# Tile 6 normalised ahead of tile 3, z sum 0 behind its rstd, and four x loads moved in SP's queue: linear attention beside a SwiGLU block on one core

## The chip, the cores and the metric

The kernel runs on one core of one Trainium2 chip. The time is the device time of one execution in microseconds. TensorE (PE) multiplies, VectorE (DVE), ScalarE (ACT) and GpSimd (POOL) do the elementwise work, and SyncE (SP) issues nearly all DMAs. Each engine works through its own list of instructions in order; semaphores make one wait for another.

## The reference: what is computed

The input x has 2048 rows of 512 features. Its rows are normalised, and two branches work on the result: linear attention with 32 heads of 16 features, and a SwiGLU network of width 1792. The output is x plus both.

```python
phi = lambda t: jnp.where(t > 0, t + 1, jnp.exp(t)) + 1e-6
xn = _layernorm(x, axis=-1)
q, k, v = split(xn @ wqkv)               # 32 heads of 16
pq, pk = phi(q), phi(k)
kv  = einsum("bhsd,bhse->bhde", pk, v)   # a sum over all rows
z   = einsum("bhsd->bhd", pk)            # a sum over all rows
o   = einsum(pq, kv) / (einsum(pq, z)[..., None] + 1e-6)
out = x + o @ wo + (silu(xn @ w_gate) * (xn @ w_up)) @ w_down
```

## The kernel before

The 2048 rows are 16 tiles of 128 rows. The first stage goes over the tiles and takes about the first 48 us of the span; the second, the feed-forward part and the output, takes the rest. The edit lies in the first stage, between 10 and 22 us.

For a tile t of the first stage:

- SP loads x (L204). Tiles 0 to 5 come alone, the others in pairs: 6/7, 8/9, 10/11, 12/13, 14/15.
- Statistics: `bns` (L297) and `agg` (L300) on VectorE give mean and variance; `eps` (L325) and `rstd_of` (L334) on GpSimd give 1/sqrt(variance + 1e-5). Each of the latter two is an instruction on one element per partition. `stat(t)` stands for the four of them.
- `xn_dve` (L314) on VectorE normalises the tile. `xn(t)` is `xn_dve(t)` with `transpose_dma(t)` (L408) behind it: SP issues a DMA that writes the transposed tile to xnT. For tile 6 of the kernel before, the two are written apart.
- `kproj`, `qproj` (L417) on TensorE: four matmuls each, with the transposed tile as weights.
- Features of k: ACT takes the exponential from the matmul's bank (L465), VectorE clips it (L484, `clip_k`) and adds the positive part (L493, `maxadd_k`).
- `gtacc` (L569) on TensorE: four matmuls that add the product of the normalised tile and its features, called G here, into four banks. The normalised tile is the weights, so they wait for `xn_dve(t)` and for the features.
- `zsum(t)` on GpSimd adds the features to zacc (L561). `zsum(0, 0)` is a copy with a change of type (L557), a "cast" in the profile.

Tiles 0 to 3 go another way, so that TensorE can begin early: their projections (L431, L444) use the tile less its mean, and ACT applies rstd afterwards (L501, L507, L519); VectorE adds the two parts of the features (L533, `first_feat`). So xn of tile 3 is needed for G only.

The order is written out by hand. A call of `K.op` or `K.dma` appends an instruction to its engine's list and works out from the names it reads and writes which semaphores it waits for. So a call that stands further up moves an instruction ahead in that engine's list alone, past everything there. TensorE's list around the edit is: G of tiles 1 and 2, k and q projections of tile 4, G of 3, projections of 5, G of 4, projections of 6, G of 5, projections of 7. From tile 5 on, a loop repeats the pattern; its statistics of tiles 10 to 15 come in the steps `STAT = {5: (10,), 6: (11,), 7: (12,), 8: (13, 14), 9: (15,)}`.

VectorE's list from the features of tile 3 on is, before the change: `first_feat(3)`, `xn_dve(3)`, `bns(7)`, `xn_dve(6)`, `agg(7)`, `bns(8)`, `agg(8)`, `clip_k(4)`, `xn_dve(7)`, `maxadd_k(4)`. GpSimd's is `rstd_of(5)`, `zsum(0, 0)`, `eps(6)`, `rstd_of(6)`, `eps(7)`, `rstd_of(7)`. SP's is the transpose of xc for tile 3, x 8/9, T4, x 10/11, T5, x 12/13, x 14/15, T6, T7, where Tn is the transpose of tile n.

Of the kernel before, what the change touches and what calls it, by code (L numbers as in the profile page):

```python
# [108 lines left out]
def bass_parallel_sum__linear_attn_block__swiglu_ffn__prompt_kernel(  # L109
# [13 lines left out]
    pe, act, dve, pool, sp = nc.tensor, nc.scalar, nc.vector, nc.gpsimd, nc.sync  # L123
    bf, f32 = dt.bfloat16, dt.float32

    with contextlib.ExitStack() as es:
# [63 lines left out]
        def bk(i):  # L190
            return ("bank", i)
# [5 lines left out]
        def rows(v, t0, n):  # L197
            if t0 < NLONE:
                return v[t0 * P:(t0 + n) * P, :].rearrange("(t p) d -> p t d", p=P)
            return v[NLONE * P:, :].rearrange("(p t) d -> p t d", t=NT - NLONE)[:, t0 - NLONE:t0 - NLONE + n, :]  # L200

        def xload(eng, h, t0, n, after=()):
            K.dma(
                eng, lambda: h.dma_start(x_sb[:, t0:t0 + n, :], rows(xin, t0, n)),  # L204
                r=list(after), w=[("x", t0 + i) for i in range(n)],
            )
# [89 lines left out]
        def bns(t):  # L296
            K.op("dve", lambda: dve.bn_stats(stats[:, t, :], x_sb[:, t, :]), r=[("x", t)], w=[("st", t)])  # L297

        def agg(t):
            K.op("dve", lambda: dve.bn_aggr(mv[:, t, :], stats[:, t, :]), r=[("st", t)], w=[("mv", t)])  # L300
# [10 lines left out]
        def xn_dve(t):  # L311
            K.op(
                "dve",
                lambda: dve.tensor_scalar(  # L314
                    out=xn_sb[:, t, :], in0=x_sb[:, t, :], scalar1=mv[:, t, 0:1], scalar2=rstd[:, t:t + 1],
                    op0=ALU.subtract, op1=ALU.mult,
                ),
                r=[("x", t), ("mv", t), ("rstd", t)], w=[("xn", t)],
            )

        def eps(t, eng):
            h = dve if eng == "dve" else pool
            K.op(
                eng,
                lambda: h.tensor_scalar(  # L325
                    out=vpe[:, t:t + 1], in0=mv[:, t, 1:2], scalar1=1e-5, scalar2=None, op0=ALU.add,
                ),
                r=[("mv", t)], w=[("vpe", t)],
            )

        def rstd_of(t):
            K.op(
                "pool",
                lambda: pool.tensor_tensor(out=rstd[:, t:t + 1], in0=vpe[:, t:t + 1], in1=nhalf[:, :], op=ALU.pow),  # L334
                r=[("vpe", t), ("nhalf",)], w=[("rstd", t)],
            )
# [40 lines left out]
        def transpose_xc(t):  # L377
            K.dma(
                "sp",
                lambda: sp.dma_start_transpose(out=xcT[:, NDC * t:NDC * (t + 1), :], in_=xc_sb[:, t, :]),  # L380
                r=[("xc", t, 0), ("xc", t, 1)], w=[("xcT", t, 0), ("xcT", t, 1)],
            )
# [22 lines left out]
        def transpose_dma(t):  # L405
            K.dma(
                "sp",
                lambda: sp.dma_start_transpose(out=xnT[:, :, t * P:(t + 1) * P], in_=xn_sb[:, t, :]),  # L408
                r=[("xn", t)], w=[("xnT", t)],
            )  # L410
# [29 lines left out]
        def proj_part(t, wname, c, pos):  # L440
            lo, b = (D, kb(t)) if wname == "wk" else (0, qb(t))
            K.op(
                "pe",
                lambda: pe.matmul(  # L444
                    banks[b], xcT[:, NDC * t + c, :], wqkv_sb[:, c, lo:lo + D],
                    start=(pos == 0), stop=(pos == NDC - 1),
                ),
                r=[("xcT", t, c // 2), (wname, c)], w=[bk(b)],
            )

        def kb(t):
            return 2 * (t % 2)

        def qb(t):
            return 2 * (t % 2) + 1

        def kproj(t):
            proj(t, kb(t), D, "wk")
# [10 lines left out]
        def exp_q(t):  # L469
            K.op(  # L470
                "act", lambda: act.activation(eq[:, t, :], banks[qb(t)], ACT.Exp),
                r=[bk(qb(t))], w=[("eq", t)],
            )

        def copy_q(t):
            K.op(
                "act", lambda: act.activation(pkq[:, t, 1, :], banks[qb(t)], ACT.Copy),
                r=[bk(qb(t))], w=[("pq", t)],
            )
# [25 lines left out]
        def first_pk(t):  # L505
            K.op(
                "act", lambda: act.activation(kpos[:, t % NE, :], banks[kb(t)], ACT.Relu, scale=rstd[:, t:t + 1]),  # L507
                r=[bk(kb(t)), ("rstd", t)], w=[("kpos", t % NE)],
            )
# [20 lines left out]
        def first_feat(t):  # L530
            K.op(
                "dve",
                lambda: dve.tensor_tensor(out=pkq[:, t, 0, :], in0=kpos[:, t % NE, :], in1=ek[:, t % NE, :], op=ALU.add),  # L533
                r=[("kpos", t % NE), ("ek", t % NE)], w=[("pk", t)],
            )

        def clip_k(t):
            clip(ek[:, t % NE, :], ("ek", t % NE))
# [14 lines left out]
        def zsum(t, e):  # L553
            pk = pkq[:, t, 0, :]
            after = [] if e is None else [("ek", e)]
            if t == 0:
                K.op("pool", lambda: pool.tensor_copy(zacc[:, :], pk), r=[("pk", t)] + after, w=[("zacc",)])  # L557
            else:
                K.op(
                    "pool",  # L560
                    lambda: pool.tensor_tensor(out=zacc[:, :], in0=zacc[:, :], in1=pk, op=ALU.add),  # L561
                    r=[("pk", t), ("zacc",)] + after, w=[("zacc",)],
                )

        def gtacc(t):
            K.op(
                "pe",
                [
                    (lambda c=c: pe.matmul(  # L569
                        banks[4 + c], xn_sb[:, t, c * P:(c + 1) * P], pkq[:, t, 0, :],  # L570
                        start=(t == 0), stop=(t == NT - 1),
                    ))
                    for c in range(NDC)
                ],
                r=[("xn", t), ("pk", t)], w=[bk(4 + c) for c in range(NDC)],
            )
# [7 lines left out]
        def xn(t):  # L584
            xn_dve(t)
            if t >= 3:
                transpose_dma(t)
# [43 lines left out]
        proj_part(1, "wq", 1, 1)  # L631
        transpose_xc(3)
        xload("sp", sp, 8, 2)
        proj_part(0, "wq", 0, 0)
        proj_part(0, "wq", 1, 1)
        first_pk(0)
# [25 lines left out]
        eps(4, "pool")  # L662
        rstd_of(4)
        xn(4)
        xload("sp", sp, 10, 2)
        agg(5)
        first_pk(1)
        first_feat(1)
# [9 lines left out]
        rstd_of(3)  # L678
        rstd_of(5)
        xn(5)  # L680
        xload("sp", sp, 12, 2)
        xload("sp", sp, 14, 2)
        bns(6)
        first_pq(2)
        proj_first(3, "wk", 1)
        first_ek(3)
        clip_k(3)
        zsum(0, 0)
        first_pk(3)
        agg(6)  # L690
        eps(6, "pool")
        first_feat(3)
        gtacc(1)
        gtacc(2)
        xn_dve(3)
        bns(7)
        kproj(4)
        rstd_of(6)
        xn_dve(6)
        agg(7)  # L700
        eps(7, "pool")
        rstd_of(7)
# [2 lines left out]
        qproj(4)  # L705
        stat(8)
        exp_q(4)
        transpose_dma(6)
        copy_q(4)
        clip_k(4)  # L710
        zsum(1, 1)
# [339 lines left out]
```

## Time and profile before

| | |
|---|---|
| median of 3 runs | 212.25 us (211.96 to 212.31) |
| the profiled execution's own time | 212.38 us |
| its span, from first to last instruction | 211.1 us |
| TensorE busy | 206.5 us, 98% |
| VectorE, ACT, GpSimd busy | 119.6, 70.9, 74.2 us |
| granted TensorE clock | 1.000 |

All stretches and instructions below come from the one profiled execution and are counted from the start of its span. A row of the timeline reads: start, duration, engine, line of the kernel, operation, output and inputs, shape, count, and in brackets how long the engine had been idle and what released it. PEld is TensorE's loading of weights, SPq the issue of a DMA by SP; the issue ends before the data have landed.

### The profile page before, as it was taken

What the parts mean: (1) busy time and instruction counts of PE and PEld (TensorE: products, weight loads), DVE (VectorE), ACT (ScalarE), POOL (GpSimd) and SP (SyncE); (2) the same over time, 40 slices, a digit from 0 to 9 for tenths busy, and PEclk for the clock granted to TensorE, in tenths of its full rate; (3) what the DMA queues carried; (4) which work ended last, traced back from release to release, by engine and by line L of the source; (5) the groups of instructions that cost most, each with busy time, mean ns of one, the idle gap of its engine ahead of it and who ended that gap; (6) DMA issues with size and microseconds to landing.
All of it is one profiled execution on the core that took longest, in us unless ns stands there. A gap on an engine that the chain in (4) does not pass through costs nothing.

```text
span 211.1 us, 2755 instructions
## 1 busy us (share of the span) xinstructions
PE 206.5 (98%) x968; PEld 95.3 (45%) x987; DVE 119.6 (57%) x246; ACT 70.9 (34%) x125; POOL 74.2 (35%) x95
## 2 busy tenths in 40 slices
PE   8999899999999999999999999999999999999996
PEld 3443444445444444444444444444444444444444
DVE  3989889434464775546374746464656535374222
ACT  4787466976443331213122312112032213121000
POOL 3638887749032444122140432231414031221200
DMA  6757444795694011210202011202021010210201
GB/s 209 202 146 162 79 99 83 201 375 191 169 363 89 3 25 25 50 25 28 51 0 50 12 33 32 50 0 50 3 50 25 26 25 28 33 44 25 50 25 53
DMA packets 30288, 16.84 MB, mean 80 GB/s; under 512 B 20929, under 2 KB 29633, under 8 KB 30273
## 3 DMA queue, kind: packets, MB, share of 16 engines
q1 hardware_dynamic: 29984, 16.39, 29.2%
q10 hardware_dynamic: 288, 0.26, 0.4%
q8 instruction: 8, 0.13, 0.3%
q14 instruction: 8, 0.06, 0.1%
HBM read 9.70 MB, written 2.10 MB: 56 GB/s over the span
## 4 chain that ended last, share of the span: by engine, by line
PE 89%; DVE 4%; DMA 3%; ACT 2%; issue 1%; POOL 1%; DVEq 0%
PE psum L771 44%; PE psum L954 23%; PE psum L417 8%; PE psum L943 7%; PE psum L569 4%; DMA xnT<-xn_sb 2%; PE psum L444 2%; DMA x_sb<-in_A_x_dram 1%; DVE pkq L533 1%; ACT ek L501 1%; ACT pkq L519 1%; PE psum L389 1%; DVE stats L297 1%; ACT kpos L507 1%; POOL prod L901 1%
## 5 line engine op out<-in xcount | busy, mean ns | idle before, releaser
L786 ACT ACTIVATE sg<-psum 128x512 bf16<-128x512 f32 x56 | 33.4, 598 | 106.8 <-PE psum L771 104.9
L771 PE MATMUL psum<-xnT,wg_sb 128*128 128x512 bf16 x222 | 57.4, 379 | 0.1
L771 PE MATMUL psum<-xnT,wu_sb 128*128 128x512 bf16 x217 | 56.0, 379 | 0.4
L901 POOL TENSOR_TENSOR prod<-pkq,zb 128x512 f32<-128x512 bf16 x16 | 18.6, 1160 | 57.8 <-DVE pkq L493 57.8
L771 PEld LDWEIGHTS psum<-xnT,wu_sb 128*128 128x128 bf16 x224 | 21.9, 98 | 26.4
L771 PEld LDWEIGHTS psum<-xnT,wg_sb 128*128 128x128 bf16 x224 | 21.9, 98 | 26.2
L967 DVE TENSOR_TENSOR out_sb<-psum,x_sb 128x512 bf16<-128x512 f32 (+2 forms) x17 | 11.2, 660 | 35.9 <-PE psum L954 35.9
L925 POOL TENSOR_TENSOR pqn<-pkq,rden 128x512 bf16<-128x512 bf16 x16 | 16.9, 1055 | 36.6 <-DVE rden L919 36.6
L792 DVE TENSOR_TENSOR pkq<-psum,sg 128x512 bf16<-128x512 f32 x28 | 19.1, 687 | 18.6 <-PE psum L771 14.1
L792 DVE TENSOR_TENSOR xn_sb<-psum,sg 128x512 bf16<-128x512 f32 x28 | 18.8, 672 | 14.2 <-PE psum L771 13.6
L954 PE MATMUL psum<-wd_sb,xn_sb 128*128 128x512 bf16 (+2 forms) x123 | 25.4, 355 | 0.2
L954 PE MATMUL psum<-wd_sb,pkq 128*128 128x512 bf16 x110 | 25.2, 379 | 0.1
L417 PE MATMUL psum<-wqkv_sb,xnT 128*128 128x512 bf16 x94 | 22.3, 379 | 0.9 <-DMA xnT<-xn_sb 0.8
L561 POOL TENSOR_TENSOR zacc<-zacc,pkq 128x512 f32<-128x512 f32 x15 | 17.3, 1155 | 5.1 <-DVE ek L484 4.6
L954 PEld LDWEIGHTS psum<-wd_sb,xn_sb 128*128 128x128 bf16 x126 | 11.8, 98 | 12.5
L954 PEld LDWEIGHTS psum<-wd_sb,pkq 128*128 128x128 bf16 x112 | 10.9, 98 | 13.2
L943 PE MATMUL psum<-m_sb,eq 128*128 128x512 bf16 (+2 forms) x67 | 16.5, 366 | 0.1
L569 PE MATMUL psum<-pkq,xn_sb 128*128 128x512 bf16 x63 | 15.9, 379 | 0.1
L417 PEld LDWEIGHTS psum<-wqkv_sb,xnT 128*128 128x128 bf16 x96 | 9.3, 98 | 12.4 <-DMA xnT<-xn_sb 1.3
L909 DVE TENSOR_REDUCE den<-prod 128x32 f32<-128x512 f32 x16 | 10.9, 683 | 5.7 <-POOL prod L901 5.7
L297 DVE BATCH_NORM_STATS2 stats<-x_sb 128x6 f32<-128x512 bf16 x16 | 10.9, 679 | 3.4 <-DMA x_sb<-in_A_x_dram 3.3
L493 DVE SCALAR_TENSOR_TENSOR pkq<-pkq,eq 128x512 bf16<-128x512 bf16 x16 | 11.1, 692 | 0.6
(65 smaller groups left out, 142.2 us busy)
## 6 DMA issues: line engine op xcount, KB each, us to landing
out_dram<-out_sb SPq DMA_DIRECT2D x15, 128.0 KB, 1.7
wg_sb<-in_B_w_gate_dram SPq DMA_DIRECT2D x2, 896.0 KB, 7.8
wu_sb<-in_B_w_up_dram SPq DMA_DIRECT2D x2, 896.0 KB, 6.0
wd_sb<-in_B_w_down_dram SPq DMA_DIRECT2D x1, 1792.0 KB, 9.7
x_sb<-in_A_x_dram SPq DMA_DIRECT2D x5, 256.0 KB, 3.1
x_sb<-in_A_x_dram SPq DMA_DIRECT2D x5, 128.0 KB, 3.3
wqkv_sb<-in_A_wqkv_dram SPq DMA_DIRECT2D x5, 128.0 KB, 3.4
wqkv_sb<-in_A_wqkv_dram SPq DMA_DIRECT2D x1, 512.0 KB, 7.6
```

What stands on the lines that cost most here:

```text
L297: K.op("dve", lambda: dve.bn_stats(stats[:, t, :], x_sb[:, t, :]), r=[("x", t)], w=[("st", t)])
L417: (lambda c=c: pe.matmul(banks[b], xnT[:, c, t * P:(t + 1) * P], wqkv_sb[:, c, lo:lo + D], start=(c == 0), stop=(c == NDC - 1),))
L561: lambda: pool.tensor_tensor(out=zacc[:, :], in0=zacc[:, :], in1=pk, op=ALU.add),
L569: (lambda c=c: pe.matmul(banks[4 + c], xn_sb[:, t, c * P:(c + 1) * P], pkq[:, t, 0, :], start=(t == 0), stop=(t == NT - 1),))
L771: (lambda c=c: pe.matmul(banks[b], w_sb[:, c, fc * P:(fc + 1) * P], xnT[:, c, C * 512:(C + 1) * 512], start=(c == 0), stop=(c == NDC - 1),))
L786: lambda: act.activation(sg[:, j % NSG, :], banks[gb], ACT.Silu),
L792: lambda: dve.tensor_tensor(out=hT(C, fc), in0=banks[ub], in1=sg[:, j % NSG, :], op=ALU.mult,),
L901: lambda: pool.tensor_tensor(out=p, in0=pkq[:, t, 1, :], in1=zb[:, :], op=ALU.mult),
L925: lambda: pool.tensor_tensor(out=pqn[:, t % NPN, :].rearrange("p (h e) -> p h e", e=DH), in0=pkq[:, t, 1, :].rearrange("p (h e) -> p h e", ...
L943: (lambda g=g: pe.matmul(dst, pqnT(t)[:, g, :], m_sb[:, g, lo:hi], start=(g == 0), stop=False,))
L954: (lambda fc=fc: pe.matmul(dst, hT(C, fc)[:, jj * P:(jj + 1) * P], wd_sb[:, fc, lo:hi], start=False, stop=(fc == NFC - 1),))
L967: lambda: dve.tensor_tensor(out=o, in0=src, in1=x_sb[:, t, lo:hi], op=ALU.add),
```

## The change

Five edits in the order of calls; no instruction is added or taken away.

- The load of x 10/11 goes from behind T4 to behind x 8/9.
- The load of x 12/13 goes from behind T5 to behind T4.
- The load of x 14/15 goes from behind T5 to behind T6.
- `rstd_of(6)` and the normalisation of tile 6 go ahead: on GpSimd eps 6 and rstd 6 stand ahead of `zsum(0, 0)`, on VectorE xn 6 stands directly behind `first_feat(3)`, ahead of xn 3 and `bns(7)`.
- The transpose of tile 6 is issued directly behind its normalisation. On SP it keeps its place between T5 and T7.

```diff
         transpose_xc(3)
         xload("sp", sp, 8, 2)
+        xload("sp", sp, 10, 2)
...
         xn(4)
-        xload("sp", sp, 10, 2)
+        xload("sp", sp, 12, 2)
...
         xn(5)
-        xload("sp", sp, 12, 2)
-        xload("sp", sp, 14, 2)
         bns(6)
...
         clip_k(3)
-        zsum(0, 0)
         first_pk(3)
         agg(6)
         eps(6, "pool")
+        rstd_of(6)
+        zsum(0, 0)
         first_feat(3)
         gtacc(1)
         gtacc(2)
+        xn(6)
+        xload("sp", sp, 14, 2)
         xn_dve(3)
         bns(7)
         kproj(4)
-        rstd_of(6)
-        xn_dve(6)
         agg(7)
...
         exp_q(4)
-        transpose_dma(6)
         copy_q(4)
```

## Prediction

> **What bounds the kernel now.** I read the page first, then who waited for whom on TensorE, then the chain that ended last, then the timeline of each engine from 8 to 26 us, where the edit lies.
>
> ```profile
> span 211.1 us, 2755 instructions
> PE 206.5 (98%) x968; PEld 95.3 (45%) x987; DVE 119.6 (57%) x246; ACT 70.9 (34%) x125; POOL 74.2 (35%) x95
> ```
>
> ```profile
> PE psum L417 <- DMA xnT<-xn_sb: 0.8, 1, 0.8
> ```
>
> TensorE is busy nearly all the time, so the only thing that an order of the other engines can win is TensorE's idle time. The list of waits on TensorE has one inside the work: 0.8 us, a projection (L417) that waits for a transposed tile. The chain and TensorE's rows show which tile.
>
> ```profile
> 17.19 0.41 DVE xn_sb L314
> ...
> 17.63 4.04 DMA xnT<-xn_sb
> ```
>
> ```profile
> 15.57 1.89 PE L417 MATMUL psum<-wqkv_sb,xnT 128*128 128x512 bf16 x8
> 17.30 1.03 PE L569 MATMUL psum<-pkq,xn_sb 128*128 128x512 bf16 x4
> 18.16 1.89 PE L417 MATMUL psum<-wqkv_sb,xnT 128*128 128x512 bf16 x8
> 19.89 1.03 PE L569 MATMUL psum<-pkq,xn_sb 128*128 128x512 bf16 x4
> 21.71 1.90 PE L417 MATMUL psum<-wqkv_sb,xnT 128*128 128x512 bf16 x8 [0.80 <-DMA xnT<-xn_sb]
> 24.31 1.89 PE L417 MATMUL psum<-wqkv_sb,xnT 128*128 128x512 bf16 x8
> ```
>
> In the order of the code these are the projections of tile 4 (15.57), G of tile 3 (17.30), projections of 5, G of 4 (19.89), projections of 6 (21.71) and of 7 (24.31). Eight matmuls follow each other in 1.73 us (18.16 to 19.89), so four take 0.86, and tile 6 could have begun at 19.89 + 0.86 = 20.75. It began at 21.71: **0.96 us** are to be won at most (the view says 0.8, because the last matmul before the gap drains). The transpose of tile 6 (T6) was issued at 17.63, right behind the normalisation of tile 6 (17.19 to 17.60), and needed 4.04 us.
>
> **The loads (edits to SP's queue).** SP's rows, and what a transpose and a load take to land:
>
> ```profile
> 10.25 0.57 SPq L204 DMA_DIRECT2D x_sb<-in_A_x_dram  x1
> 11.78 1.20 SPq L408 DMA_TRANSPOSE xnT<-xn_sb  x1
> 13.03 0.58 SPq L204 DMA_DIRECT2D x_sb<-in_A_x_dram  x1
> 14.20 1.20 SPq L408 DMA_TRANSPOSE xnT<-xn_sb  x1
> 15.44 1.05 SPq L204 DMA_DIRECT2D x_sb<-in_A_x_dram  x2
> ```
>
> ```profile
> x_sb<-in_A_x_dram SPq DMA_DIRECT2D x2, 256.0 KB, 3.1
> xnT<-xn_sb SPq DMA_TRANSPOSE x1, 2.7
> ```
>
> ```profile
> xnT<-xn_sb SPq DMA_TRANSPOSE x16, 2.5
> ```
>
> x 10/11 move from behind T4 to behind x 8/9: SP issues them from 10.82 to 11.39 in idle time, before T4 at 11.78. T4 then has two loads ahead of it in place of one. T5, one load ahead, took 2.7 against the usual 2.5, so bounds for T4 are 0 and, if it must wait out the whole second load's place, 0.57 us: it lands by 11.78 + 2.5 + 0.57 = 14.85. Its projection begins at 15.57, so this costs nothing; the cover is 0.7 us. x 12/13 take the place of x 10/11 ahead of T5, which sees what it sees now. x 14/15 go behind T6: two loads (15.44, 3.1 us each) that now lie ahead of T6 are gone, one lies ahead of T7. x 10 to 13 land earlier than now; x 14/15 land near 18.5 + 3.1 = 21.6 and are read in steps 8 and 9 of the loop, behind the projections of tile 7 (24.31): no reader waits.
>
> **Tile 6 forward, z sum 0 back (edits to VectorE and GpSimd).** The rows of VectorE, then GpSimd's, then the weight loads of G of tiles 3 and 4:
>
> ```profile
> 13.16 0.69 DVE L533 TENSOR_TENSOR pkq<-kpos,ek 128x512 bf16<-128x512 f32 x1
> ...
> 15.02 0.17 DVE L300 BATCH_NORM_AGGREGATE mv<-stats 128x2 f32<-128x6 f32 x1
> 15.39 0.94 DVE L533 TENSOR_TENSOR pkq<-kpos,ek 128x512 bf16<-128x512 f32 x1 [0.19 <-ACT kpos L507]
> 16.25 0.40 DVE L314 TENSOR_SCALAR xn_sb<-x_sb,mv,rstd 128x512 bf16<-128x512 bf16 x1
> 16.58 0.68 DVE L297 BATCH_NORM_STATS2 stats<-x_sb 128x6 f32<-128x512 bf16 x1
> ...
> 17.52 0.18 DVE L300 BATCH_NORM_AGGREGATE mv<-stats 128x2 f32<-128x6 f32 x1
> ...
> 18.73 0.41 DVE L314 TENSOR_SCALAR xn_sb<-x_sb,mv,rstd 128x512 bf16<-128x512 bf16 x1
> 19.06 0.68 DVE L493 SCALAR_TENSOR_TENSOR pkq<-psum,ek 128x512 bf16<-128x512 f32 x1
> ...
> 23.46 0.29 DVE L484 TENSOR_SCALAR ek<-ek 128x512 bf16<-128x512 bf16 x1 [0.44 <-ACT ek L465]
> ```
>
> ```profile
> 15.18 0.61 POOL L557 CAST zacc<-pkq 128x512 f32<-128x512 bf16 x1 [1.52 <-DVE ek L484]
> 15.76 0.65 POOL L325 TENSOR_SCALAR vpe<-mv 128x1 f32<-128x1 f32 x1
> 16.50 0.58 POOL L334 TENSOR_TENSOR rstd<-vpe,nhalf 128x1 f32<-128x1 f32 x1
> 17.78 0.22 POOL L325 TENSOR_SCALAR vpe<-mv 128x1 f32<-128x1 f32 x1 [0.70 <-DVE mv L300]
> 18.09 0.61 POOL L334 TENSOR_TENSOR rstd<-vpe,nhalf 128x1 f32<-128x1 f32 x1
> ```
>
> ```profile
> 17.08 0.75 PEld L569 LDWEIGHTS psum<-pkq,xn_sb 128*128 128x128 bf16 x4
> ...
> 19.80 0.62 PEld L569 LDWEIGHTS psum<-pkq,xn_sb 128*128 128x128 bf16 x4 [0.24 <-DVE pkq L493]
> ```
>
> Nothing is added or removed on VectorE; the normalisation of tile 6 (xn 6) goes ahead of that of tile 3 and of the statistics of tile 7. What counts is when it can run, for all behind it in VectorE's queue waits with it. Call its end **e**.
>
> Step 1, rstd 6. Tile 6's aggregate ends at 15.19, so eps 6 starts near 15.28 and rstd 6, 0.31 behind as with tile 7 (17.78, 18.09), near 15.59. There it meets the features of tile 3, from 15.39 on. The z sum's cast no longer runs beside these, so I give them 0.69 as at 13.16, not 0.94: they end at 16.08. Today eps 6 lies beside them and takes 0.65 in place of 0.22, ending 0.08 behind them (16.41 against 16.33). So the bounds for rstd 6 are 15.59 + 0.61 = 16.20 (not held) and 16.08 + 0.08 + (0.61 - 0.22) = 16.55 (held until the features let go). I take 16.55, the nearest row being that of eps 6.
>
> Step 2, the cast. Z sum 0 now stands right behind rstd 6 on GpSimd and waits for nothing else; GpSimd starts the next instruction 0.03 before the last ends (15.76 against 15.79), so it runs from 16.52 to 17.13. VectorE starts xn 6 some 0.11 after rstd 6 (17.08 to 17.19), at 16.66, when the cast is already running. What such a meeting costs is shown further down the trace:
>
> ```profile
> 35.04 1.24 DVE L314 TENSOR_SCALAR xn_sb<-x_sb,mv,rstd 128x512 bf16<-128x512 bf16 x1
> ```
>
> ```profile
> 34.97 1.16 POOL L561 TENSOR_TENSOR zacc<-zacc,pkq 128x512 f32<-128x512 f32 x1
> ```
>
> A normalisation that meets a z sum already running took 1.24 in place of 0.40 us and ended 0.15 behind it. So xn 6 has the bounds 16.66 + 0.40 = 17.06 and 17.13 + 0.15 = **17.28**; I take 17.28, since the features at 15.39 were also lengthened beside this very cast (0.94, not 0.69). The Trainium skill, "SBUF — State Buffer", section "Who interferes with whom", says that VectorE in a two-port mode and GpSimd exclude each other for a whole instruction and that issue order, not the kind of instruction, decides who is blocked. The row at 35.04 agrees; without that rule both meetings would cost nothing, the sum below would be a gain of 0.83, and putting the cast right behind rstd would be harmless.
>
> Step 3, behind xn 6. Xn 3 starts 0.07 before its forerunner ends, as bns 7 does now (16.58 against 16.65): 17.21 to 17.61. G of tile 3 takes xn 3 as weights; with 0.06 to the weight load and 0.09 to the matmul (as at 19.74, 19.80, 19.89) it begins at 17.76, 0.46 later than now. Bns 7 begins at 17.54 and the aggregate of tile 7 0.68 later at 18.22, 0.70 later than 17.52. The rest of the queue up to the features of tile 4 keeps its order, so these end at 19.74 + 0.70 = 20.44, and G of tile 4 begins at 20.44 + 0.15 = 20.59 (TensorE alone would be there at 19.89 + 0.46 = 20.35). Tile 6 follows at 20.59 + 0.86 = **21.45**.
>
> Step 4, T6. It is issued at 17.28 + 0.03 = 17.31 and lands at 19.8 with 2.5 us, or at 21.35 with today's 4.04: in time either way. So the wait for T6 goes, and VectorE's features of tile 4 take its place.
>
> **Sum.** 21.71 - 21.45 = 0.26 us earlier; in general 17.54 - e. Nothing gives it back later: at 23.46 VectorE has waited 0.44 us for ACT, so its 0.70 is caught up within two tiles, and the list of waits names no other wait of TensorE. The profiled execution took 212.38 us (span 211.1 and about 1.3 around it), 0.13 above the median of 212.25. 212.38 - 0.26 = 212.12, and on the scale of the medians 211.99: I forecast **212.0 us**. Less than 0.2% (0.42 us) is about what a measurement of this kernel can't tell from no change.
>
> **Rivals.** (1) The meetings on GpSimd's side cost little. With only the cast free, e = 17.06 and the gain is 0.48; with only rstd 6 free, the cast runs 16.17 to 16.78, e = 16.93, 0.61; with both, e = 16.31 + 0.40 = 16.71, 0.83; the bound is 0.96. For it speaks that instructions on one element could slip through; against it eps 6's 0.65. It gives 211.3 to 211.8.
>
> (2) The edit does not do what it says: eps 6 doesn't get ahead of the features and ends at 16.16, as it now ends behind them. Then rstd 6 ends at 16.16 + 0.09 + 0.61 = 16.86, the cast at 17.44, e = 17.59, and the gain is -0.05. Against it: the aggregate ends 0.2 us before the features start. It gives 212.3.
>
> (3) Slower: the delay of T6 passes to T7. Something made T6 need 4.04 us, and it need not have been the loads:
>
> ```profile
> q8 instruction: 1, 0.02, 32.6%
> ```
>
> ```profile
> 19.18 1.80 SPq L408 DMA_TRANSPOSE xnT<-xn_sb  x1
> ```
>
> The first row is the DMA view of the stretch from 19.4 to 19.6 us: a packet of kind "instruction" of 0.02 MB, 32.6% of 16 engines over 0.2 us, so one engine for 1.04 us, while T6's packets run out; the issue of T7 took 1.80, not 1.20. With my shift TensorE's stream, which may fetch it, is 0.46 later: 19.96 to 21.0. T6 is past by then (issued 0.3 earlier), but T7, issued at 18.73 + 0.70 + 0.41 + 0.03 = 19.87, has x 14/15 ahead of it, issued at 18.5. T7 is due 2.60 (24.31 - 21.71) behind tile 6, at 24.05. At 2.5 us it lands at 22.4; at 4.04 at 23.9, still in time. If the load's 0.57 come on top, 24.48: 0.21 slower than before; if the fetch holds the load and T7 in turn, 1.04 more. It decides from a landing 4.4 us behind the issue; I price it at 0.5 us, 212.75. The Trainium skill, "Runtime: NRT & Kernel Launch", section "Instruction fetch mechanics", has sequencers fetch 16 KiB blocks over a DMA queue of their own, mostly hidden. The 0.02 MB packet agrees in size; if it is hidden here too, this rival falls and its chance goes to the forecast.
>
> **How the numbers follow.** Forecast (e from 17.1 to 17.5) 0.47, rival 1 0.30, rival 2 0.08, rival 3 0.15. Faster by over 0.2%: rival 1 and the upper edge of the forecast (0.08), 0.38. Slower by over 0.2%: 0.11 of rival 3. The rest, 0.51, within. The range takes in most of rival 1 down to a gain of 0.85, 211.4, and the milder part of rival 3 up to 212.5.
>
> **What would show it.** In the new trace: features of tile 3 at 0.7 us, not 0.94; rstd 6 ending near 16.5; the cast beside a stretched xn 6 ending near 17.3; G of tile 3 near 17.8 and of tile 4 near 20.6, waiting for VectorE; tile 6's projections without a DMA wait at 21.4 to 21.5; T7 landed before 24. The forecast is wrong if xn 6 ends before 17.1 (then faster), or if any later projection waits for a transpose.

## The result and the profile after

The change made the kernel faster by a little: a median of 212.0 us (211.46 to 212.57, 22 runs) against 212.4 (211.96 to 212.93, 22 runs) of the kernel before on the same chips, a ratio of 0.9979 with a 95% interval of 0.997 to 0.9988, so 0.25 to 0.64 us. The profiled execution took 211.49 us, its span 210.3.

The spans of the two profiled executions differ by 0.8 us, but not all of that is the edit. The first view after is TensorE's timeline:

```profile
14.98 1.89 PE L417 MATMUL psum<-wqkv_sb,xnT 128*128 128x512 bf16 x8
17.02 1.04 PE L569 MATMUL psum<-pkq,xn_sb 128*128 128x512 bf16 x4
17.89 1.89 PE L417 MATMUL psum<-wqkv_sb,xnT 128*128 128x512 bf16 x8
19.89 1.04 PE L569 MATMUL psum<-pkq,xn_sb 128*128 128x512 bf16 x4
20.82 1.90 PE L417 MATMUL psum<-wqkv_sb,xnT 128*128 128x512 bf16 x8
22.56 1.03 PE L569 MATMUL psum<-pkq,xn_sb 128*128 128x512 bf16 x4
23.42 1.89 PE L417 MATMUL psum<-wqkv_sb,xnT 128*128 128x512 bf16 x8
```

Tile 4's projections begin at 14.98, where the profile of before has 15.57: 0.59 us arise ahead of these projections. A second execution of the kernel before, profiled later, has 14.93 there, and one of the kernel after 15.00, so this is taken as scatter of the start and not as an effect of the edit. From here on the measure is the **distance** from the start of tile 4's projections to that of tile 6's: 21.71 - 15.57 = 6.14 us before, 20.82 - 14.98 = 5.84 after, a gain of 0.30. Times of after are compared with forecast ones by adding 0.59: tile 6 at 20.82 + 0.59 = 21.41, forecast 21.45.

The list of TensorE's waits after names only two, both at the start of the kernel, ahead of the projections. The wait of 0.8 us for the transposed tile is no longer among them:

```profile
PE psum L269 <- PEq L1035: 0.8, 1, 0.8
PE psum L389 <- DVE xc_sb L361: 0.4, 1, 0.4
```

What took its place is in the timeline of all engines:

```profile
14.44 0.18 DVE L300 BATCH_NORM_AGGREGATE mv<-stats 128x2 f32<-128x6 f32 x1
14.70 0.22 POOL L325 TENSOR_SCALAR vpe<-mv 128x1 f32<-128x1 f32 x1 [1.63 <-DVE mv L300]
...
14.81 0.69 DVE L533 TENSOR_TENSOR pkq<-kpos,ek 128x512 bf16<-128x512 f32 x1 [0.20 <-ACT kpos L507]
...
15.01 0.92 POOL L334 TENSOR_TENSOR rstd<-vpe,nhalf 128x1 f32<-128x1 f32 x1
15.89 0.61 POOL L557 CAST zacc<-pkq 128x512 f32<-128x512 bf16 x1
16.03 0.93 DVE L314 TENSOR_SCALAR xn_sb<-x_sb,mv,rstd 128x512 bf16<-128x512 bf16 x2 [0.53 <-POOL rstd L334]
...
17.02 0.55 PEld L569 LDWEIGHTS psum<-pkq,xn_sb 128*128 128x128 bf16 x4 [0.64 <-DVE xn_sb L314]
...
17.60 0.18 DVE L300 BATCH_NORM_AGGREGATE mv<-stats 128x2 f32<-128x6 f32 x1
...
19.15 0.68 DVE L493 SCALAR_TENSOR_TENSOR pkq<-psum,ek 128x512 bf16<-128x512 f32 x1
...
19.89 0.55 PEld L569 LDWEIGHTS psum<-pkq,xn_sb 128*128 128x128 bf16 x4 [0.60 <-DVE pkq L493]
```

Read it downwards. The features of tile 3 take 0.69, no longer 0.94. Rstd 6 starts beside them and takes 0.92 in place of some 0.6. VectorE stands idle for 0.53 until rstd 6 is there; xn 6 and xn 3 then take 0.93 for the two, with the cast beside them. TensorE's weight loads for G of tile 3 wait 0.64 for xn 3, those for G of tile 4 0.60 for the features of tile 4. About half of that is covered by matmuls still running. Eight projections and four matmuls of G take 1.73 + 0.86 = 2.59 us, so two such rounds, 5.18, would be the distance with no wait at all. Of the 5.84 measured, TensorE still loses 0.31 ahead of G of tile 3 (16.71 to 17.02), 0.27 ahead of G of tile 4 (19.62 to 19.89) and 0.07 ahead of tile 6; the list of waits names none of these. The chain that ended last names the same path and no transpose:

```profile
15.01 0.93 POOL rstd L334
...
16.03 0.93 DVE xn_sb L314 x2
...
19.15 0.70 DVE pkq L493
19.85 0.05 issue
19.89 1.04 PE psum L569 x4
20.93 1.79 PE psum L417 x8
```

Yet T6 is not quite in time. SP's timeline, the DMA view of T6's issue alone (count, median us to landing), and TensorE's weight loads for tile 6:

```profile
9.96 1.04 SPq L204 DMA_DIRECT2D x_sb<-in_A_x_dram  x2
11.43 1.19 SPq L408 DMA_TRANSPOSE xnT<-xn_sb  x1
...
16.67 1.19 SPq L408 DMA_TRANSPOSE xnT<-xn_sb  x1
17.90 0.58 SPq L204 DMA_DIRECT2D x_sb<-in_A_x_dram  x1
19.26 1.39 SPq L408 DMA_TRANSPOSE xnT<-xn_sb  x1
```

```profile
xnT<-xn_sb SPq DMA_TRANSPOSE x1, 4.1
```

```profile
20.82 1.41 PEld L417 LDWEIGHTS psum<-wqkv_sb,xnT 128*128 128x128 bf16 x8 [0.39 <-DMA xnT<-xn_sb]
```

T6 is issued at 16.67 with no load ahead of it and still lands at 20.78. G of tile 4 would have let tile 6 begin at 19.89 + 0.86 = 20.75; the weight loads wait for T6, and tile 6 begins at 20.82. So in this profile T6 still has the last word, by 0.07 us. In the repeat (e11) T6 landed at 20.63, G of tile 4 would have let tile 6 begin at 19.91 + 0.86 = 20.77, and it began at 20.78: there VectorE's path sets it. The two tie within the scatter of T6. The packet of kind "instruction" is again there while T6 is under way, in the DMA view from 18.5 to 18.7 us (the trace puts its start at 18.55):

```profile
q8 instruction: 1, 0.02, 32.4%
```

### The profile page after: what moved, and what is told of

Its sections match the earlier page's. It is cut to its first block, busy times and chain, and to the rows that moved or that the text cites. A ratio compares the mean times of both kernels' runs of the same rounds, so it can differ in the third digit from the quotient of the medians.

```text
span 210.3 us, 2774 instructions
## 1 busy us (share of the span) xinstructions
PE 206.9 (98%) x987; PEld 94.6 (45%) x987; DVE 119.8 (57%) x246; ACT 70.9 (34%) x125; POOL 74.1 (35%) x95
## 4 chain that ended last, share of the span: by engine, by line
PE 90%; DVE 4%; POOL 3%; issue 1%; DMA 1%; ACT 0%; DVEq 0%
PE psum L770 46%; PE psum L953 23%; PE psum L417 8%; PE psum L942 7%; PE psum L569 5%; POOL rstd L334 1%; DVE stats L297 1%; DMA x_sb<-in_A_x_dram 1%; DVE xn_sb L314 1%; DVE pkq L533 1%; POOL vpe L325 1%; POOL pkq L526 1%; DVE mv L300 0%; PE psum L868 0%; PE psum L891 0%
## 5 line engine op out<-in xcount | busy, mean ns | idle before, releaser
L770 PE MATMUL psum<-xnT,wu_sb 128*128 128x512 bf16 x224 | 57.5, 379 | 0.0
L791 DVE TENSOR_TENSOR pkq<-psum,sg 128x512 bf16<-128x512 f32 x28 | 19.1, 687 | 18.5 <-PE psum L770 14.1
```

The costliest lines, as they stand in the source:

```text
L770: (lambda c=c: pe.matmul(banks[b], w_sb[:, c, fc * P:(fc + 1) * P], xnT[:, c, C * 512:(C + 1) * 512], start=(c == 0), stop=(c == NDC - 1),))
L791: lambda: dve.tensor_tensor(out=hT(C, fc), in0=banks[ub], in1=sg[:, j % NSG, :], op=ALU.mult,),
```

## The experiments

Theory A, the prediction's: what is won is set by VectorE's queue behind xn 6, through two holds, that of rstd 6 beside the features of tile 3 and that of xn 6 beside the cast; T6 is made late by something other than the loads, the packet perhaps. Theory B: the load moves alone free T6 and bring the gain. Theory C: taking tile 6 ahead alone brings it. Ratios are to the kernel before on the same chip, with their 95% intervals; the distance is that from tile 4's projections to tile 6's, from one profiled execution each. The last column is how long after T6's issue the packet began.

| kernel | ratio | distance, us | T6, issue to landing | packet after issue |
|---|---|---|---|---|
| before | | 6.14 | 4.0 | 1.9 |
| e12_before_again | | 6.38 | 4.3 | 2.0 |
| after | 0.9979 (0.997 to 0.9988) | 5.84 | 4.1 | 1.9 |
| e11_after_again | 0.9965 (0.9952 to 0.9979) | 5.78 | 3.9 | 1.8 |
| e1_loads_only | 0.9987 (0.9973 to 1.0002) | 6.41 | 4.3 | 2.2 |
| e2_norm_only | 0.9998 (0.9981 to 1.0015) | 6.24 | 4.5 | 1.7 |
| e10_cast_first | 0.999 (0.9976 to 1.0004) | 6.14 | 4.0 | 1.9 |
| e3_cast_early | 0.9965 (0.995 to 0.998) | 6.02 | 4.0 | 1.9 |
| e8_cast_behind_xn3 | 0.9971 (0.9956 to 0.9986) | 5.59 | 4.0 | 1.9 |
| e9_agg6_first | 0.9949 (0.993 to 0.9968) | 5.18 | 2.4 | 2.5 |
| e13_agg6_again | 0.9941 (0.9921 to 0.9961) | 5.18 | 2.4 | 3.3 |
| e4_fetch_moved | 0.9982 (0.9965 to 0.9999) | 6.23 | 4.1 | 1.5 |
| e5_after_fetch_moved | 0.9977 (0.9963 to 0.9991) | 5.83 | 4.1 | 2.0 |
| e7_loads_fetch | 0.9988 (0.9974 to 1.0002) | 5.33 | 3.2 | 0.9 |

The distance with no wait at all is 5.18 us. The starts of T6 and of the packet and the landings are read from the traces.

**The loads alone.** The kernel before with the load moves and nothing else. They are three (x 10/11, 12/13 and 14/15), not four as the title has it.

```diff
         xload("sp", sp, 8, 2)
+        xload("sp", sp, 10, 2)
...
         xn(4)
-        xload("sp", sp, 10, 2)
+        xload("sp", sp, 12, 2)
...
         xn(5)
-        xload("sp", sp, 12, 2)
-        xload("sp", sp, 14, 2)
...
         transpose_dma(6)
+        xload("sp", sp, 14, 2)
```

> Only the three load moves; tile 6 is normalised and z sum 0 copied where they were. Measured in the trace by the distance from the start of tile 4's projections to the start of tile 6's (6.14 us before, 5.84 after). My theory, that the 16 KB packet of kind instruction holds one of the engines that carry T6: T6 keeps its 4.0 to 4.1 us though no load is ahead of it, distance 6.1, time as before within 0.1 us. Rival, that the two loads ahead of T6 made it late: T6 lands in 2.5 us, distance 5.2, 0.9 us faster.

TensorE's timeline of that kernel, then the DMA view of T6's issue:

```profile
21.55 1.90 PE L417 MATMUL psum<-wqkv_sb,xnT 128*128 128x512 bf16 x8 [1.06 <-DMA xnT<-xn_sb]
```

```profile
xnT<-xn_sb SPq DMA_TRANSPOSE x1, 4.3
```

No load is ahead of T6 and it takes 4.3 us all the same; the wait stays (1.06). Theory B falls, and the two loads ahead of T6 were not what made it need 4 us.

**Tile 6 ahead alone.** The kernel after with the loads back in their old places.

```diff
         xload("sp", sp, 8, 2)
-        xload("sp", sp, 10, 2)
...
         xn(4)
-        xload("sp", sp, 12, 2)
+        xload("sp", sp, 10, 2)
...
         xn(5)
+        xload("sp", sp, 12, 2)
+        xload("sp", sp, 14, 2)
...
         xn(6)
-        xload("sp", sp, 14, 2)
```

> Only the move of tile 6 and of z sum 0; the loads stand where they stood before. My theory, that VectorE's queue sets the gain: distance from tile 4's to tile 6's projections about 5.8 to 5.9 us as after the whole change, 0.25 to 0.35 us faster than before. Rival, that the loads carry the gain: distance 6.1, no gain. If the loads ahead of T6 add to its landing, the distance lies between.

TensorE's and its weight loads' rows, from the timeline of that kernel:

```profile
20.12 0.55 PEld L569 LDWEIGHTS psum<-pkq,xn_sb 128*128 128x128 bf16 x4 [0.60 <-DVE pkq L493]
...
21.46 0.39 PE L417 MATMUL psum<-wqkv_sb,xnT 128*128 128x512 bf16 x1 [0.30 <-DMA xnT<-xn_sb]
```

VectorE behaves as in after and would have let tile 6 begin at 20.12 + 0.86 = 20.98. But T6, issued at 16.89, took 4.5 us, and tile 6 waited until 21.46. I had expected most of the gain here; there is none that can be told from zero. Theory C falls too: in these traces each half alone leaves TensorE waiting for T6 (1.06 and 0.30 us), and only with both does T6 land within 0.03 us of the time at which VectorE is ready. The times alone would not settle it: the interval of this ratio (0.9981 to 1.0015) overlaps that of after (0.997 to 0.9988). That the two loads cost T6 the 0.4 us by which it was slower than in after is argued from this one trace; against it stands the 4.3 of the run before, without loads.

**The cast ahead of eps 6.** The kernel after with z sum 0 back in its old place, rstd 6 and xn 6 still ahead.

```diff
         clip_k(3)
+        zsum(0, 0)
         first_pk(3)
...
         rstd_of(6)
-        zsum(0, 0)
```

> The changed kernel with the copy of z sum 0 ahead of eps 6 again, as before the change; tile 6 and the loads as changed. My theory, that rstd 6 sets when VectorE can go on: the copy runs beside the features of tile 3 (0.94 us again), eps 6 is held until they end, rstd 6 ends 1.5 us behind the start of the features where it ended 1.1 behind it, xn 3 ends 0.4 us later than in the changed kernel, distance from tile 4's to tile 6's projections about 6.2 us: no gain over before. Rival, that the order on GpSimd is of no account: 5.84.

From the timeline of all engines:

```profile
14.68 0.61 POOL L557 CAST zacc<-pkq 128x512 f32<-128x512 bf16 x1 [1.53 <-DVE ek L484]
...
14.89 0.94 DVE L533 TENSOR_TENSOR pkq<-kpos,ek 128x512 bf16<-128x512 f32 x1 [0.19 <-ACT kpos L507]
...
15.26 0.65 POOL L325 TENSOR_SCALAR vpe<-mv 128x1 f32<-128x1 f32 x1
15.99 0.57 POOL L334 TENSOR_TENSOR rstd<-vpe,nhalf 128x1 f32<-128x1 f32 x1
16.67 0.74 DVE L314 TENSOR_SCALAR xn_sb<-x_sb,mv,rstd 128x512 bf16<-128x512 bf16 x2 [0.84 <-POOL rstd L334]
```

This is rival 2's order of events: the features at 0.94 and eps 6 at 0.65 as before, rstd 6 at 15.99, xn 6 ending near 16.67 + 0.41 = 17.08. Tile 4 starts 0.50 earlier here than in the profile of before, so that is 17.58 on its scale; the rival said 17.59, and a gain of -0.05. The distance came out at 6.14, just that of before. So with rstd 6 and xn 6 ahead but the cast in its old place the gain in distance is gone. The cast's move is needed; that it is enough by itself no run shows.

**The cast earlier still.** The kernel after with the cast between rstd 3 and rstd 5, so that it meets neither rstd 6 nor xn 6.

```diff
         rstd_of(3)
+        zsum(0, None)
         rstd_of(5)
...
         rstd_of(6)
-        zsum(0, 0)
```

> The changed kernel with the copy of z sum 0 taken away from behind rstd 6: it runs before rstd 5, when its input is already there. My theory, that this copy holds xn 6: xn 6 takes 0.4 us and ends 0.2 us earlier, distance from tile 4's to tile 6's projections 5.6 to 5.65 us, 0.45 to 0.5 us faster than before, if T6 still needs 4.1 us (it then lands at the same moment). Rival, that only rstd 6 and not the copy holds it: no difference to the changed kernel, 5.84.

From the timeline of all engines:

```profile
14.81 0.69 DVE L533 TENSOR_TENSOR pkq<-kpos,ek 128x512 bf16<-128x512 f32 x1
...
14.88 0.70 POOL L325 TENSOR_SCALAR vpe<-mv 128x1 f32<-128x1 f32 x1 [1.49 <-DVE mv L300]
15.66 0.57 POOL L334 TENSOR_TENSOR rstd<-vpe,nhalf 128x1 f32<-128x1 f32 x1
16.34 0.74 DVE L314 TENSOR_SCALAR xn_sb<-x_sb,mv,rstd 128x512 bf16<-128x512 bf16 x2 [0.84 <-POOL rstd L334]
```

The pair of normalisations fell from 0.93 to 0.74, as expected. But the cast at its new place, 11.19, met the features of tile 1 (1.01 us, where after has 0.67), VectorE ran later, and the features of tile 3 now started 0.07 ahead of eps 6, which was held (0.70, not 0.22). The distance is 6.02, not the expected 5.6: a hold taken away at one place came back at another. The time does not follow the distance here: the ratio of 0.9965 is 0.7 us, more than after gains, though the distance is longer. This edit also changes what runs ahead of tile 4's projections, which begin earliest of all in this profile (14.86), and the distance does not cover that; from one profile it stays open.

**The cast behind xn 3.** The kernel after with the cast behind the normalisation of tile 3, made to wait for it.

```diff
-                K.op("pool", lambda: pool.tensor_copy(zacc[:, :], pk), r=[("pk", t)] + after, w=[("zacc",)])
+                K.op("pool", lambda: pool.tensor_copy(zacc[:, :], pk), r=[("pk", t), ("xn", 3)] + after, w=[("zacc",)])
...
         rstd_of(6)
-        zsum(0, 0)
...
         xn_dve(3)
+        zsum(0, 0)
```

> The changed kernel with the copy of z sum 0 made to wait until tile 3 is normalised, so that it can't run beside xn 6 and nothing else moves. My theory, that it holds xn 6: xn 6 and xn 3 take 0.74 us together instead of 0.93, distance 5.6 to 5.65 us (5.84 in the changed kernel), T6 issued 0.2 us earlier and landing about when TensorE needs it. Rival, that the copy costs nothing: 5.84.

From the timeline of all engines:

```profile
15.07 0.92 POOL L334 TENSOR_TENSOR rstd<-vpe,nhalf 128x1 f32<-128x1 f32 x1
16.10 0.74 DVE L314 TENSOR_SCALAR xn_sb<-x_sb,mv,rstd 128x512 bf16<-128x512 bf16 x2 [0.53 <-POOL rstd L334]
...
16.91 0.61 POOL L557 CAST zacc<-pkq 128x512 f32<-128x512 bf16 x1 [0.91 <-DVE xn_sb L314]
```

Only the cast moved, rstd 6 is held as in after (0.92), and the two normalisations take 0.74 in place of 0.93: the cast cost xn 6 **0.19 us**, where the prediction's two bounds lie 0.22 apart. The distance fell to 5.59, as expected.

**Rstd 6 ahead of the features.** The same, with the aggregate, eps and rstd of tile 6 also placed ahead of the clip of tile 3.

```diff
         bns(6)
+        agg(6)
+        eps(6, "pool")
+        rstd_of(6)
         first_pq(2)
...
         first_pk(3)
-        agg(6)
-        eps(6, "pool")
-        rstd_of(6)
         first_feat(3)
```

> As the kernel before in this call, and tile 6's aggregate, eps and rstd ahead of the clip of tile 3's exponential, so that rstd 6 starts before the features of tile 3 do. My theory, that a GpSimd instruction that reads while these features run is held until they end: rstd 6 takes 0.6 us instead of 0.92, xn 6 starts right behind the features and ends near 15.9 us, TensorE waits neither for VectorE nor for T6, distance 5.2, 0.9 us faster than before. Rival, that rstd 6 is long for another reason: rstd 6 0.9 us, distance 5.6.

Rows of the timelines (the matmul rows are those of TensorE's own), then the DMA view of T6's issue:

```profile
15.00 0.57 POOL L334 TENSOR_TENSOR rstd<-vpe,nhalf 128x1 f32<-128x1 f32 x1
15.01 0.72 DVE L533 TENSOR_TENSOR pkq<-kpos,ek 128x512 bf16<-128x512 f32 x1 [0.23 <-ACT kpos L507]
15.19 1.89 PE L417 MATMUL psum<-wqkv_sb,xnT 128*128 128x512 bf16 x8
15.66 0.73 DVE L314 TENSOR_SCALAR xn_sb<-x_sb,mv,rstd 128x512 bf16<-128x512 bf16 x2
...
20.37 1.89 PE L417 MATMUL psum<-wqkv_sb,xnT 128*128 128x512 bf16 x8
```

```profile
xnT<-xn_sb SPq DMA_TRANSPOSE x1, 2.4
```

Rstd 6 starts 0.01 us ahead of the features of tile 3, not 0.2 behind them, and takes 0.57, not 0.92. The hold cost **0.35 us**, just the gap between the prediction's bounds (16.20 and 16.55). T6, issued at 16.08, took 2.4 us, and the distance is 5.18: TensorE waits for nothing in this stage. The Trainium skill, "SBUF — State Buffer", section "Who interferes with whom", says that the order of issue decides which of the two engines is blocked; this pair of kernels agrees for GpSimd, 0.57 against 0.92 with the order turned by 0.2 us. That VectorE is blocked in its turn this run does not show: the features, started 0.01 behind rstd 6, took 0.72 against 0.69.

**The packet moved.** To push the packet off T6, the warm-up matmuls at the start were issued as twice as many of half the size, so that TensorE's stream of instructions would reach any given count earlier: on the kernel before (e4), on the kernel after (e5), and on the loads-only kernel (e7).

```diff
-        fill(8, 512)
+        fill(16, 256)
```

> The kernel before, with the 8 filling matmuls of 512 columns at the start written as 16 of 256: the same columns, 8 matmuls and 8 weight loads more, so that whatever is fetched by TensorE's count of instructions comes 16 instructions, some 1.7 us, earlier. My theory, that a fetch for TensorE makes T6 late: the 16 KB packet starts near 17.8 us instead of 19.5, T6 lands in about 2.5 us, tile 6 starts at 20.75, distance 5.2, 0.9 us faster than before. Rival, that T6 is late for another reason (loads, its place): T6 4.0 us, distance 6.1, no gain.

> The changed kernel with the filling matmuls at the start written as 16 of 256 columns, so that what TensorE fetches by count comes some 1.7 us earlier. In the changed kernel SP's queue is idle there, so the 16 KB packet should run near 16.6 us and be through before T6's packets (from 17.9). My theory, that VectorE's queue sets the changed kernel: T6 lands in 2.5 us, no TensorE wait for it is left, but the distance from tile 4's to tile 6's projections stays 5.75 to 5.85 us. Rival, that T6's late landing sets it: distance 5.2 us, 0.6 us faster than the changed kernel. Second rival, that the packet has nothing to do with T6: T6 4.1 us.

> Only the load moves, with the filling matmuls as 16 of 256 columns; tile 6 and z sum 0 as before. With the load moves alone T6 still took 4.3 us and the distance was 6.4. My theory: the packet runs before T6's, T6 lands in 2.5 us, VectorE is not behind, distance 5.2, 0.9 us faster than before. Rival, that the order on VectorE is needed as well: distance 5.8. Second rival, that the packet is no cause: 6.1 to 6.4.

In e4 and e5 the packet began 1.5 and 2.0 us after T6's issue, and T6 took 4.1 us in both. Counted from tile 4's projections the packet shifted by -0.4 and +0.1 us, not away from T6, so these two say nothing of the cause; e5 only gives the distance of after once more (5.83). The interval of e4's ratio ends just below 1 though its distance lies between the two of before; what accounts for that is not known. In e7 it shifted by -1.3 us and came 0.9 us after the issue, and T6 took 3.2, where the loads-only kernel without this edit has 2.2 and 4.3. Part of such a shift may be scatter: the two profiles of the fastest kernel put the packet 3.4 and 4.2 us behind the start of tile 4's projections. VectorE's order is that of before in e7, and tile 6 began only 0.15 us behind the end of G of tile 4 (19.78 + 0.86 = 20.64), released by T6. The timeline of TensorE in e7, and the DMA view of T7's issue:

```profile
20.79 1.90 PE L417 MATMUL psum<-wqkv_sb,xnT 128*128 128x512 bf16 x8
...
23.79 1.89 PE L417 MATMUL psum<-wqkv_sb,xnT 128*128 128x512 bf16 x8 [0.24 <-DMA xnT<-xn_sb]
```

```profile
xnT<-xn_sb SPq DMA_TRANSPOSE x1, 3.9
```

But now T7, with x 14/15 ahead of it, took 3.9 us and tile 7 waited: 3.00 us behind tile 6, not 2.60, so 0.40 of 0.81 went back. The issue of x 14/15 took 0.97 us there, not 0.58, while the packet ran (18.39 to 19.35). That fits rival 3's mechanism, a load and T7 delayed one after the other.

**Repeats.** The kernels after and before, and the fastest one, profiled and timed again on another chip.

> The changed kernel once more, for the spread of one profiled execution: distance from tile 4's to tile 6's projections 5.8 to 5.9 us, T6 4.0 to 4.2 us, landing within 0.1 us of the time at which VectorE lets TensorE go on; 0.2 to 0.45 us faster than before.

> The kernel before once more, for the spread of one profiled execution: distance 6.1 to 6.4 us (6.14 in the first profile, 6.41 with the load moves alone), T6 4.0 to 4.3 us.

> The fastest version so far (tile 6's aggregate, eps and rstd ahead of the clip of tile 3, copy of z sum 0 behind xn 3, loads as changed) once more: distance 5.2 us, 0.9 to 1.2 us faster than before, faster than the changed kernel by 0.6 us or more.

TensorE's timeline in the second profile of the kernel before:

```profile
14.93 1.89 PE L417 MATMUL psum<-wqkv_sb,xnT 128*128 128x512 bf16 x8
...
21.31 1.90 PE L417 MATMUL psum<-wqkv_sb,xnT 128*128 128x512 bf16 x8 [1.03 <-DMA xnT<-xn_sb]
```

T6 took 4.3 us there, and the distance is 6.38, 0.24 more than in the first profile. That one execution took 211.98 us all the same, 0.40 less than the first, since tile 4's projections began 0.64 earlier. The kernel after came out at 5.78, the fastest kernel at 5.18 again. So the edit's gain in distance is 0.30 us from the first pair of profiles and 0.60 from the second, and the gains in the medians, 0.4 us (ratio 0.9979) and 0.7 (0.9965), lie about there.

## Why the prediction came out right

- **What bounds it, and the path.** Right but for 0.07 us. After the change the features of tile 4 stand where the wait for T6 stood, as the weight loads' row at 19.89 shows (0.60, released by VectorE). But the row at 20.82 still has T6 as releaser, and a later wait for a transpose was one of the prediction's own signs of being wrong. It is met in this profile, if only by 0.07 us; in the repeat T6 was there in time.
- **The loads.** T4 with two loads ahead took 3.1 us, the upper of the two bounds (2.5 + 0.57), and landed at 14.6, due at 14.98; with one load ahead it took 2.5 and 3.0 in the two profiles of before, so how much the second load costs is not shown. T7 took 2.6 (issued at 19.26, due at 23.42). No reader waited. What the step left out is that the moves might be needed: it gave them no value, and e2 without them has no gain in its one profile.
- **Step 1, rstd 6.** It ended at 15.93, with the 0.59 added 16.52; forecast 16.55. The hold is real: turning the order takes 0.35 away.
- **Step 2, the cast.** It ran from 15.89 to 16.50, so to 17.09 (forecast 17.13), and held xn 6. Without it the pair takes 0.19 less. The 0.11 from rstd 6 to xn 6 was taken from a row that did not show it, for VectorE was still at bns 7 there (16.58 + 0.68 = 17.26); after the change the step is 0.10 (15.93 to 16.03), so nothing came of it.
- **Step 3.** Xn 3 ended at 16.96, so 17.55 (17.61); G of tile 3 began at 17.61 (17.76), the aggregate of tile 7 at 18.19 (18.22), G of tile 4 at 20.48 (20.59), tile 6 at 21.41 (21.45).
- **Step 4, T6.** "In time either way" failed by a hair in the first profile and held in the second. The case with 4.04 us was the one that applied (4.1 and 3.9 us): T6 landed at 20.78, with the 0.59 added 21.37 (forecast 21.35), but VectorE's limit came at 21.34 and not at 21.45. The 2.5 us that one might hope for without the loads did not come; e1 shows the same.
- **The sum.** 212.0 was the median, and that it agrees to the tenth is in part luck. The forecast subtracted 0.26 from a median of 3 runs, 212.25; over 22 runs the kernel before has 212.4, and the gain is 0.4. Tile 6 came within 0.04 us of its forecast place because two errors offset each other: VectorE's path was done 0.11 earlier (21.34 against 21.45), and T6 took 0.07 back. The term that was mis-sized is the wait that goes. The forecast took it from one execution, in which T6 needed 4.04 us; in the second it needed 4.27 and the distance was 0.24 longer. A base that waits longer than the one profile showed would explain why the gain on the medians, 0.4 to 0.7 us, is above 0.26; two profiles do not prove it. The prediction also held that a change of 0.2% could hardly be told from none; 22 runs of each kernel did tell it (0.997 to 0.9988).
- **The rivals.** Rival 1 (the meetings cost little) is refuted: they cost 0.19 and 0.35 us, and without both the distance falls by 0.96 against the first profile of before, the bound that the prediction named. Rival 2 did not happen but its price was right (e10). Rival 3 did not happen in after; in e7 tile 7 did wait for T7.

**A faster kernel.** With the cast behind xn 3 and rstd 6 ahead of the features of tile 3 the median is 211.12 us against 212.38, a ratio of 0.9949 (0.993 to 0.9968), and on the other chip 211.36 against 212.39, 0.9941 (0.9921 to 0.9961): 1.0 to 1.3 us faster than the kernel before by the medians, of which the distance explains 0.96 to 1.20.

**What stays open.** What makes T6 late. In the twelve profiles in which the packet began 0.9 to 2.2 us after T6's issue, T6 took 3.2 to 4.5 us; in the two in which it began 2.5 and 3.3 us after, T6 had landed and took 2.4. Those two differ from the others in VectorE's order as well, and e7, which differs from e1 only in the warm-up matmuls, brought T6 down to 3.2 and not to 2.4. In the two with 2.4 us (e9 and e13) the packet fell on T7 instead, beginning 0.07 us before its issue and 0.7 us after, and T7 took 3.2 and 3.8 us where the kernel after has 2.6; TensorE did not wait for it. Against it stands T7 in e7, 3.9 us though the packet was over 0.4 us before its issue. So the packet fits as one cause, but it is argued and not shown. What decides when the packet comes is open too: the same edit shifted it by -0.4, +0.1 and -1.3 us, and without any edit it moved by 0.8 us between the two profiles of the fastest kernel.

## What to carry to other kernels

Before moving work ahead to start a transfer earlier, follow what the moved instructions meet on the engine beside them: here two instructions on GpSimd, one of them on a single element per partition, decided 0.5 us of a possible 1. A wait read from one profile is one draw; profile the base a second time before taking its length as the gain. And try the halves of an edit alone before calling one of them the cause: here neither half showed a gain that could be told from zero.

## What the runs showed of the hardware that was not expected

- A DMA transpose of one tile took 2.4 us in some places and 3.9 to 4.3 in others with no load ahead of it (e1, after and its repeat). In after fifteen of the sixteen completions that the trace records for T6 came at 18.93 to 19.08 and the last only at 20.78, and e11, e3 and e8 show one straggler in the same way; in the kernel before and in e1 all sixteen came late, within 0.1 us of each other. The Trainium skill, "Runtime: NRT & Kernel Launch", section "Instruction fetch mechanics", calls the cost of crossing a 16 KiB boundary in the instructions mostly hidden; if the packet is the cause, it was not hidden here: T6 took 1.5 to 1.9 us more beside a packet of 1.0.
- The start of tile 4's projections lay at 15.57 and 14.93 us in the two profiles of the kernel before, and between 14.86 and 15.81 in all fourteen profiles, a scatter as large as the effect under study. A distance between two points around the edit shows that effect more cleanly than the span.
